# Bits issued from Pool, six operand tiles, new planner figures for a transpose, one hash in one pass, last store in halves

## The chip, the cores and the metric

The kernel runs on one core of one Trainium2 chip. The metric is the device time of one execution in microseconds (us). Before the change it is 277.95 us (median of three runs, 274.41 to 279.09). An execution that took over 1.5% more than the fastest of the same kernel is marked slow; the others are called fast. Every ratio below is the mean time of one kernel's fast runs over the mean time of the other kernel's fast runs of the same rounds on the same chip, so it is not quite the ratio of the medians that stand beside it. The interval behind it is a 95% interval.

## The reference

Hashed attention for 4 batches of 8 heads (768 tokens, head size 64), followed by a feed-forward network (FFN) with a maximum over three first layers:

```python
q_bits = (einsum('bhsd,dk->bhsk', q, proj) > 0)      # 6 bits; the same for k
mask = q_bucket[:, :, :, None] == k_bucket[:, :, None, :]
scores = where(mask, scale * q @ k.T, -1e9)          # softmax, then @ v
...                                                  # heads side by side: x is 3072 x 512
h = maximum(maximum(x @ w1, x @ w2), x @ w3)         # 512 -> 768
out = h @ w_out                                      # 768 -> 512
```

## The kernel before

Work goes by pairs of heads, four pairs in each batch; I write (1,2) for pair 2 of batch 1. A pair's q and k are loaded by SyncE, split into two fp16 parts by ScalarE and VectorE (tile `s`), and transposed into the operand tile `T`: the first six pairs on TensorE, the other ten by a DMA transpose from SBUF to SBUF. TensorE then hashes `T` (tile `hps`); VectorE makes bits of the hash. The bits go SBUF to HBM (`dr<-bt`) and from there into spare rows of `T` (`T<-dr`), so that the score matmul itself carries the mask. I call those two copies a bounce.

```python
def xbar(b, pr, e):                                   # the DMA transpose
    nc.sync.dma_start_transpose(operand(b, pr)[:], S16[b, pr][:].rearrange("p a d -> p (a d)"))
def bit_out(b, pr, e):
    ...
    nc.sync.dma_start(drs[b, pr][:].rearrange("n r t -> r n t"), bts.pop((b, pr))[:])
def bit_in(b, pr, e):
    nc.sync.dma_start(T[b, pr][D : D + NBITS, :, :], ...)
```

The order of the instructions on each engine is not written down. A list scheduler makes it at build time. Each task has a planned time on its engine; a DMA has a planned transfer time too (`xfer`). When an engine is free in the plan, the ready task of best priority is emitted. The plan says that a DMA has landed after its time on the engine, 0.3 us (2.4 for Pool), the transfer, and `POST` = 1.2 us.

```python
ev = [add(("SP", 2.0), p0 + 2, both_rs, lambda e: xbar(b, pr, e), xfer=4.3, take=("T",))]
...
hm = add(("PE", 1.3 if b == 0 else 0.67), p0 + 4, ev + [mp], lambda e: hash_mm(b, pr, (0, 2), e), take=("mm",))
...
stage = {(0, 3): [(1, 0)], (1, 0): [(1, 1), (1, 2)], (1, 1): ["o"]}   # weight loads, issued by Pool
# "o": nc.gpsimd.dma_start(wout_sb[:], ...) waits until the bits of (1,1) are in
```

So the plan takes a transpose to have landed 2.0 + 0.3 + 4.3 + 1.2 = 7.8 us after its issue, at the earliest (the plan lets transfers through one at a time), and places the hash of that pair accordingly. The last weight load, W_out, is 768 KB in fp16, cast by the DMA from 1536 KB of fp32, issued by Pool.

The softmax here doesn't subtract the row's maximum and nothing guards it: scores larger than these inputs give would overflow.

## Time and profile before

| what | before |
|---|---|
| median of the runs | 277.95 us |
| span of the profiled run (fast) | 272.9 us |
| TensorE busy | 260.2 us, 95% |
| hash waiting for transposes | 0.5 us |
| score waiting for bits | 2.3 us |
| half-clock intervals of TensorE inside the run | one, 3.4 us at 97 |

The first thing to read is TensorE's 95%: time can be won or lost only where TensorE stands still or has its clock halved. The prediction below shows the lines for this. (A chain there is the work that ended last, followed back from the last instruction, at each step to what released it. A DMA lands with its last completion record.) One more view is needed for what came later: SyncE's issues around 54 us (columns: start, how long the instruction held the queue, what was issued).

```profile
49.49 0.33 SPq L337 DMA_DIRECT2D dr<-bt  x1
54.62 4.36 SPq L271 DMA_TRANSPOSE T<-s  x1
59.15 0.35 SPq L340 DMA_DIRECT2D T<-dr  x1
...
63.90 5.12 SPq L445 DMA_TRANSPOSE xT<-xn  x1
```

The bits of (1,1) go out, the transpose of (1,2) is issued while they travel, then the bits come in. W_out is issued by Pool at 62.77, after that transpose has landed (61.01 by the completion records of the trace, 6.39 us after issue). The last line is the transpose of the FFN's input, half as large. It was issued 1.1 us after W_out and landed 11.19 us later; the six others of its kind landed in 3.65 to 5.26. Nothing waited for it at once, and I passed over it when I predicted.

### The profile page before, as it was taken

To read this page: it belongs to the slowest core of one execution; us is meant where nothing else is said; L and a number is where in the kernel's file an instruction comes from. 1 tells how busy PE (TensorE), PEld (TensorE's weight loads), DVE (VectorE), ACT (ScalarE), POOL (GpSimd) and SP (SyncE) were. 2 spreads that over 40 slices of the span, in tenths; PEclk is the share of its full clock that TensorE was granted. 3 is DMA by queue.
4 is the path that set the end of the run, shared out by engine and by line. 5 is a ranking of instruction groups with operands and counts; after the bars stand their busy time and mean duration, and the time that the engine had idled before them with its cause. 6 is when DMAs were issued, how large, how long until landed. Compare 5 with 4: busy or idle time off the path is not lost.

```text
span 272.9 us, 7413 instructions
## 1 busy us (share of the span) xinstructions
PE 260.2 (95%) x3034; PEld 175.1 (64%) x3034; DVE 176.7 (65%) x392; ACT 196.0 (72%) x282; POOL 37.9 (14%) x56
## 2 busy tenths in 40 slices
PE   7999989999999699899999999999999999999993
PEld 7878767667657365567667676666666656565551
DVE  4998598958958569766999466454356715354350
ACT  5797899999856178898999889998889432322322
POOL 1170042604303033030333000000000000000000
PEclk9999999999999979999999999999999999999998
DMA  7996496989999969999799950211250050120303
GB/s 206 350 221 112 137 268 180 148 143 324 204 288 237 155 234 234 260 204 278 193 208 263 198 116 8 34 26 41 77 60 4 0 155 20 40 79 0 115 0 116
DMA packets 67216, 40.51 MB, mean 148 GB/s; under 512 B 47982, under 2 KB 64110, under 8 KB 67182
## 3 DMA queue, kind: packets, MB, share of 16 engines
q1 hardware_dynamic: 63150, 36.90, 55.1%
q0 software_dynamic: 3952, 3.15, 7.9%
q8 instruction: 23, 0.38, 0.6%
q14 instruction: 11, 0.09, 0.1%
q10 hardware_dynamic: 80, 0.00, 0.0%
HBM read 25.72 MB, written 6.84 MB: 119 GB/s over the span
## 4 chain that ended last, share of the span: by engine, by line
PE 76%; DMA 11%; DVE 6%; ACT 4%; issue 1%; SPq 1%; ACTq 0%
PE ps L466 32%; PE sc L383 19%; PE po L480 10%; PE av L401 10%; DMA T<-s 6%; ACT AT L389 3%; DMA T<-dr 3%; DVE s L262 3%; PE hps L300 2%; DMA q<-in_q_dram 2%; PE tps L281 1%; PE hps L298 1%; DVE s L257 1%; DVE T L193 1%; ACT s L255 1%
## 5 line engine op out<-in xcount | busy, mean ns | idle before, releaser
L389 ACT ACTIVATE AT<-sc 128x768 f16<-128x768 f32 x192 | 146.1, 813 | 16.2 <-PE sc L383 15.1
L466 PE MATMUL ps<-xT,w_sb 128*128 128x384 f16 x576 | 107.1, 327 | 0.7 <-ACT ht L191 0.6
L383 PE MATMUL sc<-T 128*128 128x384 f16 x384 | 93.7, 327 | 3.5 <-DMA T<-dr 2.3
L475 DVE TENSOR_TENSOR ht<-ht,ps 128x384 f16<-128x384 f16 x96 | 53.0, 552 | 47.3 <-PE ps L466 43.8
L401 PEld LDWEIGHTS <-AT 128*128 128x128 f16 x1152 | 60.2, 98 | 24.3 <-issue 1.2
L466 PEld LDWEIGHTS <-w_sb 128*128 128x128 f16 x576 | 52.5, 98 | 30.9 <-issue 1.5
L401 PE MATMUL av<-vone,AT 128*128 128x65 f16 x1152 | 66.3, 193 | 0.3 <-DVE t L418 0.3
L383 PEld LDWEIGHTS <-T 128*128 128x128 f16 x384 | 30.1, 98 | 14.5 <-DMA T<-dr 2.9
L191 ACT CAST ht<-ps 128x384 f16<-128x384 f32 x30 | 14.4, 478 | 32.9 <-DVE ht L475 20.6
L480 PE MATMUL po<-wout_sb,ht 128*128 128x512 f16 x144 | 33.4, 379 | 0.0
L191 ACT COPY osb<-po 128x512 f32<-128x512 f32 x23 | 13.5, 585 | 18.5 <-PE po L480 18.4
L480 PEld LDWEIGHTS <-ht 128*128 128x128 f16 x144 | 13.6, 98 | 14.4
L418 DVE TENSOR_TENSOR t<-av,mv 128x390 f32<-128x390 f32 x32 | 17.9, 560 | 7.0 <-PE av L401 7.0
L351 POOL TENSOR_TENSOR vt<-v 128x384 f32<-128x384 f32 x12 | 12.9, 1073 | 63.8 <-DMA v<-in_v_dram 63.6
L262 DVE SCALAR_TENSOR_TENSOR s<-k,s 128x384 f16<-128x384 f32 x32 | 20.9, 665 | 0.7 <-ACT s L255 0.5
L262 DVE SCALAR_TENSOR_TENSOR s<-q,s 128x384 f16<-128x384 f32 x32 | 19.4, 620 | 2.9 <-ACT s L255 2.7
L193 DVE CAST ht<-ps 128x384 f16<-128x384 f32 x18 | 10.0, 556 | 15.2 <-PE ps L466 15.2
L437 DVE TENSOR_TENSOR xn<-t,rr 128x384 f16<-128x384 f32 x32 | 18.7, 584 | 1.1
L281 PE MATMUL tps<-iden,s 128*128 128x128 f16 x168 | 13.5, 219 | 1.5 <-DVE s L262 0.6
L281 PEld LDWEIGHTS <-s 128*128 128x128 f16 x168 | 10.5, 98 | 3.1 <-DVE s L262 1.8
L191 ACT CAST vone<-v 128x768 f16<-128x768 f32 x12 | 10.1, 839 | 0.0
L300 PEld LDWEIGHTS <-T 128*128 128x128 f16 x288 | 8.6, 96 | 1.9 <-DMA T<-s 1.1
(53 smaller groups left out, 141.8 us busy)
## 6 DMA issues: line engine op xcount, KB each, us to landing
v<-in_v_dram SPq DMA_DIRECT2D x16, 384.0 KB
out_dram<-osb SPq DMA_DIRECT2D x24, 256.0 KB
q<-in_q_dram SPq DMA_DIRECT2D x15, 384.0 KB
k<-in_k_dram SPq DMA_DIRECT2D x15, 384.0 KB
w_sb<-in_moe_w_dram POOLq DMA_DIRECT2D x6, 384.0 KB, 6.5
wout_sb<-in_moe_w_out_dram POOLq DMA_DIRECT2D x1, 768.0 KB, 11.5
dr<-bt SPq DMA_DIRECT2D x15, 36.0 KB
T<-dr SPq DMA_DIRECT2D x15, 36.0 KB
```

The lines of the kernel that those rows point to most:

```text
L191: nc.scalar.copy(o, i)
L262: nc.vector.scalar_tensor_tensor(out=s[:, a0:a1, D : 2 * D], in0=raw_view(n, b, pr, heads), scalar=QS, in1=s[:, a0:a1, 0:D], op0=AluOp.mul ...
L281: nc.tensor.transpose(p16[:, c * P : (c + 1) * P], S16[b, pr][:, a0 + c, :], iden[:])
L300: nc.tensor.matmul(o, T[b, pr][:, a, :], PAB[:], start=True, stop=True)
L383: nc.tensor.matmul(sc[:, i, 0:HQ], t[:, NA2 + hh * NCH + 2 * j + i, :], t[:, hh * NCH + hf * CH : hh * NCH + (hf + 1) * CH, :], start=True ...
L389: nc.scalar.activation(AT[:], scs.pop(u)[:, :, 0:HQ], ActFn.Exp, bias=EXP_BIAS, scale=EXP_SCALE)
L401: nc.tensor.matmul(av[:, o : o + D + 1], AT[:, i, c * P : (c + 1) * P], vones[b % 2][:, 2 * pr + hh, 2 * j + i, 0 : D + 1], start=slot == ...
L418: nc.vector.tensor_tensor(out=t[:, :, :, 0 : D + 1], in0=av[:, :, :, 0 : D + 1], in1=mv, op=AluOp.add)
L437: nc.vector.tensor_tensor(out=xv, in0=t[:, :, :, 0:D], in1=rr[:].to_broadcast([P, 2, CH, D]), op=AluOp.mult)
L466: nc.tensor.matmul(ps[:, 0:HQ], w_sb[i][:, jc, fb * P : (fb + 1) * P], xTs[b, hf][:, jc, :], start=jc == 0, stop=jc == NJ - 1)
L475: nc.vector.tensor_tensor(out=ht[:], in0=ht[:], in1=ps[:, 0:HQ], op=AluOp.max)
L480: nc.tensor.matmul(ps[:], hts[b, hf, fb][:, c * P : (c + 1) * P], wout_sb[:, fb, :], start=fb == 0, stop=fb == NF - 1)
```

## The change

The intent: take the bits of the later pairs off SyncE, where they queue behind transposes; tell the planner that a transpose occupies SyncE for 4.3 us; use less SBUF for operand tiles; halve the matmuls of one hash; shorten the tail.

```diff
-    OSB = 3
+    OSB = 5
-    opnd = ... bufs=8        # and "T": 8 in the plan
+    opnd = ... bufs=6        # and "T": 6
-        K = NBITS if b == 0 else 2 * NBITS
+        summed = 4 * b + pr < 3          # (0,3) is now hashed in one pass
+        K = NBITS if summed else 2 * NBITS
-        nc.sync.dma_start(drs[b, pr]...          # bit_out, bit_in
+        ENG[e].dma_start(drs[b, pr]...
+    POOL_FROM = 6
-            ev = [add(("SP", 2.0), p0 + 2, both_rs, lambda e: xbar(b, pr, e), xfer=4.3, take=("T",))]
+            ev = [add(("SP", 4.3), p0 + 2, both_rs, lambda e: xbar(b, pr, e), xfer=0.4, take=("T",))]
-        hm = add(("PE", 1.3 if b == 0 else 0.67), ...
+        hm = add(("PE", 1.3 if 4 * b + pr < 3 else 0.67), ...     # hash bits: 0.3 -> 0.62 likewise
+        mover = ("POOL", 0.9) if 4 * b + pr >= POOL_FROM else ("SP", 0.65)
-        bo = add(("SP", 0.65), ...                                # and bi
+        bo = add(mover, ...
-        for c in range(CH):
+        for c in range(CH) if (b, hf) != (B - 1, 1) else (0, 1, 2.1, 2.6):    # last output tile in halves
... (cut: the bodies for halves of an output tile)
```

The planned landing of a transpose falls from 7.8 to 4.3 + 0.3 + 0.4 + 1.2 = 6.2 us. Since transfers pass one at a time in the plan, other DMAs behind a transpose are planned sooner too.

## The prediction

> **What bounds the kernel now.** I read the page's shares first, then the time stretch by stretch, then the chain of waits, then the groups inside the stretches that lose time, last the order of issues on SyncE. The shares:
>
> ```profile
> PE 260.2 (95%) x3034; PEld 175.1 (64%) x3034; DVE 176.7 (65%) x392; ACT 196.0 (72%) x282; POOL 37.9 (14%) x56
> ```
>
> TensorE is busy 95% of the span, so a change elsewhere can only give back what TensorE loses. To see where it loses, I cut the span in stretches (columns: stretch and its length, then PE, PEld, DVE, ACT, POOL busy us with instruction counts, granted clock, DMA share, GB/s):
>
> ```profile
> 10.00:25.00 15.00, 14.43 (x301) 12.33 (x299) 14.42 (x32) 12.42 (x18) 5.86 (x7) 1.00 1.02 239
> 25.00:50.00 25.00, 23.28 (x390) 17.80 (x387) 20.01 (x50) 23.33 (x34) 6.86 (x11) 1.00 0.69 182
> 50.00:85.00 35.00, 34.70 (x392) 22.80 (x389) 26.81 (x60) 29.70 (x44) 10.00 (x14) 1.00 1.02 219
> 85.00:100.00 15.00, 12.35 (x128) 7.59 (x126) 10.09 (x22) 5.16 (x9) 2.05 (x4) 0.90 0.90 200
> 110.00:125.00 15.00, 13.98 (x202) 9.60 (x201) 10.93 (x25) 13.56 (x21) 2.33 (x3) 1.00 1.17 239
> 125.00:160.00 35.00, 35.00 (x475) 24.32 (x473) 28.12 (x63) 31.68 (x45) 6.78 (x9) 1.00 1.01 226
> 160.00:268.60 108.60, 108.56 (x952) 66.98 (x950) 51.92 (x104) 64.61 (x96) 0.00 (x0) 1.00 0.17 45
> ```
>
> Busy time flatters, since matmul ends are modelled. So I counted the matmuls of each stretch and multiplied by the pace at which the chain shows them end to end: 0.327 us for two of score, 0.65 for four of the first FFN layer, 0.184 for six of attend, 1.29 for six of the second layer, 0.58 for 24 of the one-pass hash. From 160 on this gives 108.9 us of work in 108.6 us: full, nothing to win. 50 to 85 and 125 to 160 are full too. What is lost: 1.0 us in 10 to 25, 4.0 in 25 to 50, **4.3 in 85 to 100** (10.7 of work in 15), **1.8 in 110 to 125**. Together 11.1 us, beside about 9 of start-up and the tail.
>
> The two bold losses in the chain (start, length, what):
>
> ```profile
> 90.30 0.71 PE ps L466 x4
> 91.02 4.86 DMA T<-dr
> 95.93 0.82 PE sc L383 x4
> ...
> 102.93 8.01 DMA T<-s
> 110.99 0.76 PE hps L300 x24
> ...
> 113.96 9.39 DMA T<-s
> 123.40 0.76 PE hps L300 x24
> ```
>
> At 95.9 the first score of the eighth pair (batch 1, pair 3) waits for its hash bits, which travel SBUF to HBM and back. After that idling the 5-us stretch 95 to 100 runs at a granted clock of 0.69 with 2.7 us of work in it; TensorE was idle 0.93 us in that stretch, so the clock alone took about 1.3. Why the bits are late stands in SyncE's issue order:
>
> ```profile
> 78.44 6.35 SPq L271 DMA_TRANSPOSE T<-s  x1
> 84.84 1.43 SPq L489 DMA_DIRECT2D out_dram<-osb  x2
> 86.38 0.56 SPq L337 DMA_DIRECT2D dr<-bt  x1
> 87.05 3.87 SPq L271 DMA_TRANSPOSE T<-s  x1
> 91.02 0.41 SPq L340 DMA_DIRECT2D T<-dr  x1
> ```
>
> The outbound bits stand behind a transpose that holds the queue for 6.35 us and behind two stores; their completion record comes 2.75 us after issue (89.1), but the inbound copy stands behind another transpose of 3.87 us and then needs 4.86 us itself. An undisturbed bounce in this trace (out at 162.6, in at 164.1) lands after 1.45 and 2.33 us. The hash waits at 111.0 and 123.4 are another thing: they wait for the transposes themselves.
>
> **What the Trainium skill says.** "DMA: Bandwidth & Descriptors", section "Issuing engines are not separate DMA queues": starting DMAs from several engines saves only the starting sequencer's time, usually a small thing. The trace differs in size: a transpose holds SyncE for 3.7 to 6.4 us, so here that time is the point. The same page, section "Queues, rings and completion order": SP has its own row of rings and each DMA engine takes turns between rows, so bits from Pool need not stand behind SyncE's packets; no trace yet shows that. "SBUF — State Buffer", section "SBUF: two separate sides": Pool's descriptors can be starved while VectorE holds the shared port in a two-port mode. The seven weight loads issued from Pool took 0.75 to 0.92 us, beside a VectorE that was mostly busy: no sign of it. "TensorE: Matmul & The Clock Gate", Part 1: an idle TensorE is put on half clock, in windows of 3413 ns. Agrees: the trace's clock record has one half-clock interval of 3.413 us at 97.
>
> **The change part by part.** I compared the emitted orders and measured, in TensorE work at the paces above, how much lies between the transpose of a pair's bits and that pair's first score.
>
> *Bounces from Pool (pairs 6 to 15), and a schedule that knows that a transpose holds SyncE 4.3 us.* 20 issues leave SyncE (327 + 287 ns a pair, 6.1 us in all) and cost Pool about 20 x 0.79 = 16 us (the mean of a weight load's issue), on an engine busy 38 of 273: not on the path. Pair (1,3), the one that stalls, had 10.9 us between bits and score and gets 16.0; (1,2) had 14.4 and gets 11.5; every later one has 15.7 or more. Pair (1,1) stays on SyncE but no longer has a transpose between its two copies. Bounce needed: 0.5 VectorE + 0.8 issue + some 3 landing + 0.8 issue + some 3 landing, about 8 us. So (1,3) no longer waits: I credit its idle 2.0 us and 1.3 of clock. The 0.9 left of the 4.3 is FFN evictions, kept. **-3.3.**
>
> *Six operand tiles for eight.* In a later batch four tiles are live and two prefetch. A tile is freed a batch-half before its successor is needed, so no score starves, but it gates the transposes: (2,2), (2,3), (3,2) and (3,3) start their transpose 5 to 14 us of TensorE work later than their split. Between the earliest start of a transpose and its hash the new order leaves 8.5 to 13.9 us, seven of ten under 10. A transpose lands 6.4 to 9.4 us after issue in this trace. The old order had 9.2 to 12.6 and lost 1.8. I expect slightly more such waits: **+0.9.**
>
> *Hash of (0,3) in one pass.* 24 matmuls for 48: 1.18 us becomes 0.58. VectorE pays 300 + 307 ns instead of 299. Both fall in 25 to 50, where ScalarE is busy 23.3 of 25 and TensorE already has 4 us spare, so I count half: **-0.3.**
>
> *Five output tiles, last store in halves.* Five tiles: no wait on an output tile is on the path. Halves: six matmuls of 512 become twelve of 256, the same time. The last eviction, 585 ns for 512 columns against 478 for 384 on the same engine, so 0.84 ns a column, falls to about 0.37: 0.2 saved. The last store carries half (2.0 us landing for 256 KB, 1.45 for 36 KB): 0.3 saved. **-0.5.**
>
> Sum: -3.3 + 0.9 - 0.3 - 0.5 = -3.2 us.
>
> **Rivals.**
> First, hash waits take the place of the score wait. For it: TensorE takes its work in order, the hash slack is shorter than before for most pairs, and DMA is near full from 65 to 160 (share about 1). Against: bounces leave SyncE, so transposes issue sooner. If seven transposes lose 0.7 us each, it is +4.9 less the 1.8 there is: the gain is gone, near 277.5.
> Second, Pool's order becomes the new blockage. Pool waits 63.6 us for value loads in nine waits, up to 12.8; a bounce put behind such a sum inherits the wait. In the new order four of the Pool bounces have the sum of a later pair between out and in. For (1,2), with 11.5 us, a late value tile would bring the old stall back: 3 us, near 277. Against: that tile's load stands directly behind the first transpose in SyncE's order, 17 us of TensorE work before its sum, and the later pairs have slack to spare.
> Third, everything works: no waits after 50, all 6.1 us of the two bold losses back, plus 0.8: 7 us, near 270. ScalarE speaks against the whole of it: 31.7 of 35 busy in 125 to 160, so work pulled forward meets an engine that is nearly full.
>
> **Range and chances.** The three runs before are 274.41, 277.95 and 279.09, the profiled one 274.82 with a span of 272.9. Waits on DMA are what can differ from one run to the next, and so can the clock window that follows a wait; fewer waits should help the slow runs more. From the median 277.95, minus 3.2, minus about 1.5 for that: **273.2**. Low 269.8 (third rival and quiet runs), high 277.2 (first or second). Faster by over 2% means under 272.4: 0.38. Within 2%: 0.58. Slower needs both rivals at once: 0.04.
>
> **What would show it.** In the profile after: no transfer of bits on the chain before the scores between 85 and 100, no half-clock interval inside the run, and lost TensorE time there near 1 us. Bits issued by Pool in about 0.8 us, landing in 2 to 4. Waits of the hash for transposes 2 to 3 us in sum; over 5 and the first rival won. Pool waiting for a value tile with bits queued behind it, and a score waiting for them: the second. The last store's eviction near 0.37 us. I am wrong if the chain shows a transpose wait of over 1.5 us, or if 125 to 160 is no longer full.

## The result

| | before | changed |
|---|---|---|
| median | 277.32 us (4 runs, 274.41 to 279.09) | 290.69 us (4 runs, 288.24 to 294.36) |
| ratio of fast runs | | 1.0489 [1.0352, 1.0627]: slower |
| span of the profiled run | 272.9 us | 292.6 us |

The changed kernel is 4.9% slower, where I had expected 1.7% faster. Its profiled run took 294.36 us and counts as slow (2.1% above the fastest run); its fast runs took 288.24, 290.45 and 290.93. So some 4 us of the profile's span are more than usual. What I read from it returns in fast profiles of the experiments.

The shares of the changed kernel:

```profile
PE 264.4 (90%) x3016; PEld 177.4 (61%) x3016; DVE 175.7 (60%) x388; ACT 199.9 (68%) x288; POOL 50.9 (17%) x76
```

TensorE's share fell from 95% to 90%. The stretches of the changed kernel that answer to those in the prediction (stretch and its length, then PE, PEld, DVE, ACT and POOL busy, granted clock, DMA share, GB/s):

```profile
25.00:50.00 25.00, 22.80 (x372) 17.60 (x371) 19.89 (x49) 23.79 (x34) 5.10 (x9) 1.00 0.60 170
50.00:85.00 35.00, 21.70 (x235) 13.94 (x233) 19.63 (x42) 20.45 (x29) 10.46 (x15) 0.88 1.13 164
85.00:100.00 15.00, 14.57 (x148) 9.03 (x149) 5.93 (x15) 6.54 (x11) 2.01 (x3) 0.83 0.66 152
110.00:125.00 15.00, 13.38 (x169) 9.01 (x168) 12.22 (x27) 12.25 (x17) 4.22 (x7) 1.00 0.65 118
125.00:160.00 35.00, 32.02 (x397) 21.50 (x396) 25.28 (x55) 27.40 (x39) 10.62 (x15) 0.95 1.04 226
```

The stretch 50 to 85 was full before and now holds 235 matmuls instead of 392. It is the hole. Counting the matmuls at their chain pace, as in the prediction, TensorE loses here:

| stretch | lost before, us | lost after, us |
|---|---|---|
| 10 to 50 | 5.0 | 5.1 |
| 50 to 85 | 0.3 | 15.6 |
| 85 to 100 | 4.3 | 2.5 |
| 100 to 125 | 1.7 | 2.4 |
| 125 to 160 | -0.4 | 5.1 |

The sum goes from 10.9 to 30.7 us, a difference of 19.8; the spans differ by 19.7. So this table has all of the loss. Waits of TensorE in the changed kernel (us in total, times, longest):

```profile
PE hps L301 <- DMA T<-s: 13.9, 4, 7.7
```

Before, this line read 0.5 us, once. Most of the rest of the loss is clock: TensorE's clock record has half-clock intervals of 6.8 us at 73.2 and 83.4 and of 3.4 us at 138.0, each in or behind one of these waits, against one of 3.4 us before. Half of the TensorE busy time inside these intervals, an estimate of what they cost, is 6.0 us against 1.7. Small waits moved as well; that of scores for ScalarE's tile `AT` grew from 0.9 to 3.7 us. The chain of the changed kernel around the three waits (start, length, what):

```profile
49.83 6.93 DMA dr<-bt
...
66.16 2.34 DMA q<-in_q_dram
68.50 16.88 DMA T<-s
85.43 0.81 PE hps L301 x24
...
127.97 8.87 DMA T<-s
136.89 0.76 PE hps L301 x24
```

A transpose that took 6.4 to 9.4 us before needs 16.88 us here. SyncE's and then Pool's issues in the changed kernel:

```profile
56.90 0.29 SPq L341 DMA_DIRECT2D T<-dr  x1
...
58.75 7.35 SPq L271 DMA_TRANSPOSE T<-s  x1
...
68.50 13.28 SPq L271 DMA_TRANSPOSE T<-s  x1
```

```profile
60.25 1.23 POOL L647 DMA_DIRECT2D wout_sb<-in_moe_w_out_dram  x1 [0.28 <-issue]
```

The order has flipped. Before, the transpose of (1,2) stood between the two copies of the bits of (1,1). Now it stands behind both and behind the next pair's loads, and W_out follows 1.5 us after it, because W_out too starts when those bits are in:

```
before:   bits(1,1) out   T(1,2)          bits(1,1) in   loads(1,3)  loads(2,0)   | Pool: W_out
changed:  bits(1,1) out   bits(1,1) in    loads(1,3)     T(1,2)  | Pool: W_out |  loads(2,0)  T(1,3)
```

By the completion records the transpose of (1,2) landed after 17.5 us, W_out after 18.91 (11.46 before), three loads after 12.7 to 13.7, and the transpose of (1,3), which could not be issued before the first one let go, after 16.88. Two cuts of 5 us from that time:

```profile
70.00:75.00 5.00, 0.00 (x0) 0.00 (x0) 0.00 (x0) 0.00 (x0) 0.00 (x0) 0.82 1.39 106
75.00:80.00 5.00, 3.70 (x46) 2.66 (x47) 0.76 (x3) 1.02 (x2) 0.00 (x0) 0.50 1.24 275
```

For 5 us no engine does anything while DMA is full (share 1.39) and moves only 106 GB/s. Then TensorE comes back at half clock.

### The profile page after: what moved, and what is told of

Read it like the earlier page. It is cut to its first block, busy times and chain, and to the rows that moved or that the text cites.

```text
span 292.6 us, 7393 instructions
## 1 busy us (share of the span) xinstructions
PE 264.4 (90%) x3016; PEld 177.4 (61%) x3016; DVE 175.7 (60%) x388; ACT 199.9 (68%) x288; POOL 50.9 (17%) x76
## 4 chain that ended last, share of the span: by engine, by line
PE 57%; DMA 23%; DVE 12%; ACT 3%; issue 2%; SPq 1%; ACTq 0%
PE ps L467 24%; PE sc L384 12%; DMA T<-s 11%; PE po L485 10%; DMA q<-in_q_dram 8%; PE av L402 7%; DVE s L262 5%; DMA dr<-bt 3%; DVE s L257 2%; DVE ht L476 2%; ACT s L255 1%; PE hps L301 1%; ACT AT L390 1%; PE tps L281 1%; DVE xn L438 1%
## 5 line engine op out<-in xcount | busy, mean ns | idle before, releaser
L390 ACT ACTIVATE AT<-sc 128x768 f16<-128x768 f32 x192 | 146.0, 812 | 19.7 <-PE sc L384 18.9
L467 PE MATMUL ps<-xT,w_sb 128*128 128x384 f16 x576 | 109.0, 330 | 1.3 <-DVE ht L476 0.9
L384 PE MATMUL sc<-T 128*128 128x384 f16 x384 | 95.2, 331 | 4.3 <-ACT AT L390 3.7
L402 PEld LDWEIGHTS <-AT 128*128 128x128 f16 x1152 | 61.8, 99 | 25.8 <-issue 2.9
L402 PE MATMUL av<-vone,AT 128*128 128x65 f16 x1152 | 67.7, 195 | 0.0
L384 PEld LDWEIGHTS <-T 128*128 128x128 f16 x384 | 30.7, 98 | 15.7 <-issue 5.3
L485 PE MATMUL po<-wout_sb,ht 128*128 128x512 f16 (+1 forms) x150 | 33.4, 370 | 0.0
L262 DVE SCALAR_TENSOR_TENSOR s<-q,s 128x384 f16<-128x384 f32 x32 | 20.8, 656 | 8.5 <-ACT s L255 8.3
L191 ACT COPY osb<-po 128x512 f32<-128x512 f32 (+1 forms) x24 | 13.6, 567 | 17.0 <-PE po L485 16.8
L301 PE MATMUL hps<-PAB,T 128*128 128x12 f16 x312 | 9.8, 169 | 14.1 <-DMA T<-s 13.9
L438 DVE TENSOR_TENSOR xn<-t,rr 128x384 f16<-128x384 f32 x32 | 19.7, 615 | 1.1
L255 ACT ACTIVATE s<-q 128x768 f16<-128x768 f32 (+1 forms) x10 | 7.8, 778 | 15.8 <-DMA q<-in_q_dram 13.9
L301 PEld LDWEIGHTS <-T 128*128 128x128 f16 x312 | 9.1, 97 | 15.5 <-DMA T<-s 14.9
## 6 DMA issues: line engine op xcount, KB each, us to landing
wout_sb<-in_moe_w_out_dram POOLq DMA_DIRECT2D x1, 768.0 KB, 18.9
```

The costliest lines, as they stand in the source:

```text
L191: nc.scalar.copy(o, i)
L262: nc.vector.scalar_tensor_tensor(out=s[:, a0:a1, D : 2 * D], in0=raw_view(n, b, pr, heads), scalar=QS, in1=s[:, a0:a1, 0:D], op0=AluOp.mul ...
L301: nc.tensor.matmul(o, T[b, pr][:, a, :], PAB[:], start=True, stop=True)
L384: nc.tensor.matmul(sc[:, i, 0:HQ], t[:, NA2 + hh * NCH + 2 * j + i, :], t[:, hh * NCH + hf * CH : hh * NCH + (hf + 1) * CH, :], start=True ...
L390: nc.scalar.activation(AT[:], scs.pop(u)[:, :, 0:HQ], ActFn.Exp, bias=EXP_BIAS, scale=EXP_SCALE)
L402: nc.tensor.matmul(av[:, o : o + D + 1], AT[:, i, c * P : (c + 1) * P], vones[b % 2][:, 2 * pr + hh, 2 * j + i, 0 : D + 1], start=slot == ...
```

## The experiments

Sixteen kernels ran. My theories, in the order in which I formed them: first, that the one-pass hash flips the order, and that the flip makes the transposes meet W_out; the rivals were Pool's bounces and the six tiles. Then, that the new planner figures (4.3 and 0.4 us) place each hash too soon after its transpose. Where an expectation uses letters, A is the first theory and C the one of the figures; others are the rivals it describes.

### First round: is it the flip?

**e1: the changed kernel without the one-pass hash.**

```diff
-        summed = 4 * b + pr < 3        # and the planned times likewise
+        summed = b == 0
```

> The changed kernel with the hash of batch 0 pair 3 put back to two passes, all else as changed. Built orders show why this is asked: that one part flips SyncE's order, so that the transpose of pair (1,2) stands in front of the inbound bits of (1,1) again instead of behind them and behind three loads, and the output-weight load from Pool comes after it. Theory A (the flipped order, with the output-weight load running into the transposes, costs the time): hash waits for transposes fall from 13.9 us to under 4, no transpose lands later than 10 us after issue, time 272 to 278 us. Theory B (six tiles or bounces from Pool cost the time): it stays near 288 to 291.

Measured: 280.23 us, ratio 1.0194 [1.0093, 1.0294], profile span 278.0. SyncE's order is that of before again, and no operand transpose takes over 9.3 us. So more than half of the loss is gone. But the hash waits are not under 4 us as I had expected. They are 8.6 us in five waits:

```profile
PE hps L301 <- DMA T<-s: 8.6, 5, 3.3
```

With the order restored, something else still makes hashes wait.

**e2: the kernel before with the one-pass hash alone.** The edit is the `summed` part of the diff above.

> The kernel before with only the one-pass hash of batch 0 pair 3. Theory A: the same flip of SyncE's order, so slow by itself: 284 to 294 us, with a transpose landing 14 us or more after issue near 60 us of the span. Theory B: within 1% of before, about 277 us.

Measured: 279.74 us, ratio 1.0142 [1.0066, 1.0217]. The flip is there: the transpose of (1,2) at 57.19 landed after 14.22 us, that of (1,3) at 66.33 after 13.54. One hash wait of 5.8 us follows, and 6.8 us of half clock at 70.5. This single part of the change, which I had booked as a gain of 0.3 us, costs 1.4%. It costs less than I expected here (284 to 294 us): with the old figures no other hash waits for a transpose in its profile.

**e3: the changed kernel with W_out issued earlier,** between the other weight loads near 38 us, in the same order otherwise.

```diff
+        if (i, half) == (0, 1):                      # in load_w
+            nc.gpsimd.dma_start(wout_sb[:], ...)
-                           lambda e: nc.gpsimd.dma_start(wout_sb[:], ...),
+                           lambda e: None,
```

> The changed kernel, same order of everything on all engines, except that Pool issues the output-weight load (768 KB) about 22 us earlier, right behind the weight load at 37 us, away from the transposes. Theory A1 (it is the overlap of this load with the transposes): transposes near 58 and 68 us land 6 to 9 us after issue, hash waits under 5 us, time 274 to 280. Theory A2 (it is the late transpose itself: inbound bits and loads ahead of it, two transposes in a row): transposes still land late, time stays 285 or more.

Measured: 287.31 us, but three of four runs were slow and the one fast run took 282.63, so there is no ratio. The first two transposes landed in 8.6 and 8.9 us, without the collision, but they were issued only at 63.2 and 71.6: the earlier load pushed the other weight loads and the bits of (1,1) back. The time of this run is confounded and I do not use it.

**e4: the kernel before with W_out moved into the first transpose,** by the same edit at a later weight load.

> The kernel before, same order, except that Pool issues the output-weight load about 14 us earlier, right behind two weight loads at 47 us, so that it is in flight when the transpose of (1,2) is issued at about 54.6 us. Theory A1: that transpose lands 11 us or more after issue instead of 6.4, the hash of (1,2) waits, time 3 to 10 us longer (280 to 287). Theory A2: transpose lands in under 8 us, time within 1% of before.

Measured: 275.37 us, ratio 0.9992 [0.9924, 1.006]. The edit missed: W_out ran from 49.42 to 60.40 and the transpose was issued at 57.11, so they shared 3 us, and the transpose landed after 7.91. It says nothing on a full overlap. The two on their own follow in e11.

### Second round: one part at a time

**e5: the kernel before with the new figures alone.**

```diff
-            ev = [add(("SP", 2.0), ..., xfer=4.3, take=("T",))]
+            ev = [add(("SP", 4.3), ..., xfer=0.4, take=("T",))]
```

> The kernel before with only the planner's figures for a transpose changed (SyncE 4.3 us and 0.4 us of transfer instead of 2.0 and 4.3), so the order that the changed kernel's planner makes, all else as before. In its built order the hash follows the earliest start of its transpose by 8.0 to 8.8 us of TensorE work for six of ten pairs (9.2 to 12.6 before). Theory C (the new figures plan the hash before the transposes land): the hash waits for transposes more: TensorE's waits on transposes rise from 0.5 us to 4 or more, time 278 to 283. Rival D (figures harmless, hash flip is all): within 1% of before.

Measured: 284.56 us (one of the four runs slow), ratio 1.0298 [1.0208, 1.0388]. The profiled run is fast. Its waits:

```profile
PE hps L301 <- DMA T<-s: 7.0, 4, 2.9
```

Its transposes land in 5.5 to 9.6 us (6.4 to 9.4 before). No transfer became much slower; the hash was placed nearer. Counted in the traces at the paces above, TensorE's work between the issue of a transpose and its hash is 4.9 to 8.8 us here, 6.5 in the mean, where it was 6.2 to 9.5 and 8.2. (The slack in the expectation is counted in the built order from the splits on.) Behind two of the waits the clock halves, at 78.5 and 157.0. Two numbers in the planner cost 3.0%.

**e6: the kernel before with Pool's bounces alone** (`POOL_FROM = 6`).

> The kernel before with only the bounces of pairs 6 to 15 issued from Pool. Theory C and D: the score wait and half-clock interval near 96 us go, bits land in 3 to 5 us, time 1 to 2% shorter, 270 to 274. Theory B (bounces from Pool cost the time): 280 or more, with scores waiting for bits or Pool busy behind value tiles.

Measured: 277.64 us, ratio 1.0067 [0.9991, 1.0143]. The score wait near 96 is gone, and the stretch 85 to 100 loses 2.1 us instead of 4.3. But 100 to 125 loses 6.0 instead of 1.7. What the profile wins in one stretch it loses in the next, and the time is not the 270 to 274 us that I had expected. A new wait and a half-clock interval at 109.8 stand there:

```profile
PE av L402 <- DVE t L419: 1.5, 1, 1.5
```

One hash also waits 1.7 us for its transpose, against 0.5 before.

**e7: the kernel before with six operand tiles alone.**

> The kernel before with only six operand tiles for eight. Theory C and D: within 1% of before (275 to 278); the stall near 96 us stays, since its pair comes before the tiles bind. Theory B' (six tiles cost the time): 280 or more, with score or hash waits after 100 us.

Measured: 276.56 us, ratio 1.0008 [0.9911, 1.0105]. The tiles cost nothing that the runs resolve, about 1% either way. The other half of the expectation failed: the stall near 96 us did not stay, though the bits still go through SyncE and stand behind a transpose. SyncE's issues, and TensorE at 95 to 100 (busy all of it, at full clock):

```profile
88.89 0.47 SPq L338 DMA_DIRECT2D dr<-bt  x1
89.46 4.08 SPq L271 DMA_TRANSPOSE T<-s  x1
93.64 0.41 SPq L341 DMA_DIRECT2D T<-dr  x1
```

```profile
95.00:100.00 5.00, 5.00 (x63) 3.39 (x61) 3.44 (x8) 3.24 (x6) 0.00 (x0) 1.00 0.82 240
```

e7's order differs a little from that of before. But e4, e12 and e15 have SyncE's order of before unchanged, and TensorE's too but for e12's shorter hash. Scores wait for bits 2.3 us in the profile before, and not at all, 0.5 and 0.4 us in these three; none has a half-clock interval near 97. This is e12's line:

```profile
PE sc L384 <- DMA T<-dr: 0.5, 1, 0.5
```

And of the 28 executions of the kernel before that were timed beside the experiments, 23 were granted a mean clock of 0.996 or more. One half-clock interval of 3.4 us in a span of 273 takes the mean to 0.994, so these 23 had none inside. The stall that the bounces from Pool were to remove belonged to the profiled execution more than to the kernel.

**e8: the changed kernel with two-pass hash and the old figures (2.0 and 4.3).** What is left are Pool's bounces, six tiles, five output tiles and the halved store.

> The changed kernel with two parts put back: the two-pass hash of batch 0 pair 3 and the old planner figures for a transpose; bounces from Pool, six tiles, five output tiles and the split last store stay. Theory C with A: both harmful parts gone, hash waits under 2 us in sum, no half-clock interval inside the run, time 270 to 274, faster than before. Theory B: still 278 or more.

Measured: 277.02 us, ratio 1.0025 [0.994, 1.0109]. The whole loss has gone, with the hash waits (0.4 us). Taken one at a time, the parts sum to nearly the whole: flip 1.4, figures 3.0, rest 0.25, together 4.7% against 4.9% measured. They do not sum in every grouping: e1 holds the figures and the rest and costs 1.9%, less than the figures alone in e5, though the intervals overlap. That the bounces bring nothing shows here too: I had expected 270 to 274 us and no half-clock interval inside the run, and there is one at 109.8. The chain of e8:

```profile
89.74 1.57 SPq L271
...
91.38 5.04 DMA q<-in_q_dram
...
101.67 0.81 DVE s L262
...
108.27 0.48 DVE t L419
...
108.80 0.34 PE av L402 x6
```

The bits no longer stand behind the transpose; the loads of the next pairs still do. The load at 91.38 follows a transpose that held SyncE. Its splits on VectorE then come so late that VectorE reaches the addition that frees the attend bank only at 108.27, and TensorE waits. I took it that this lateness did not show in the kernel before because TensorE stood still for the bits in that time. e4 speaks against that: in the order of before, its TensorE does not wait for bits, and by the same count it loses only about 2.5 us in 100 to 125. What makes VectorE late here stays open.

### Third round: separate the figures, the overlap and the operation

**e9: the changed kernel with one figure changed,** the planned transfer of a transpose.

```diff
-            ev = [add(("SP", 4.3), ..., xfer=0.4, take=("T",))]
+            ev = [add(("SP", 4.3), ..., xfer=4.3, take=("T",))]
```

> The changed kernel with one figure changed: the planner is told 4.3 us of transfer for a transpose in place of 0.4 (SyncE stays at 4.3), so a hash is planned 10 us after its transpose is issued in place of 6. The one-pass hash and its flipped order stay. Theory C: the waits of the hash for transposes after 100 us go, and those on the first two shrink; TensorE's waits on transposes fall from 13.9 us to 3 to 8, time 278 to 284, in place of 290.7. If the figure is not the cause, it stays at 287 or more.

Measured: 277.2 us (one run slow), ratio 1.0035 [0.9939, 1.0131]. SyncE's order in e9 still has the flip:

```profile
57.49 6.47 SPq L271 DMA_TRANSPOSE T<-s  x1
...
65.77 11.61 SPq L271 DMA_TRANSPOSE T<-s  x1
```

These two transposes still land after 14.6 and 13.7 us, W_out after 16.0. Yet the hash waits are

```profile
PE hps L301 <- DMA T<-s: 0.9, 1, 0.9
```

because more TensorE work stands between the issue of a transpose and its hash: 8.8 to 12.5 us counted in the trace, against 3.3 to 8.5 in the changed kernel, and over 12 for the two slow ones. This is the most telling run: the slow landing need not become a hash wait; with the short figure it does. It is not free where it stands: by the same count TensorE still loses about 6 us in 50 to 85, in other waits of up to 1.2 us. The whole time is that of before within the interval, up to 1.3% more.

**e10: two-pass hash and 4.3 + 2.7,** meant as a version to beat both kernels.

> Candidate to beat both: the changed kernel with the two-pass hash put back and a transpose planned as SyncE 4.3 us and 2.7 us of transfer, near what the traces show (8.5 us from issue to landing with the planner's fixed parts). Theory C with A: hash waits under 1 us, 271 to 276, not slower than before. If loads that bunch up on SyncE and late VectorE work bind, as near 105 us in the run with the old figures, it is again within 1% of before.

Measured: 275.08 us, ratio 0.9975 [0.9895, 1.0054]: the same as before. It has no half-clock interval inside the run, and still no gain. Its largest wait is for the addition that frees the attend bank (2.8 us in three waits).

**e11: the collision by itself.** A kernel that only issues loads of W_out and the same transpose, phase after phase, each phase after the one before has landed, three times over. Its output is wrong, which doesn't matter for the time. It is one run of unknown state, 240.47 us; the phases are compared within it.

```python
for _ in range(3):
    phase([], True)                     # the transpose alone
    phase(["pool_cast"], False); phase(["pool_cast"], True)     # W_out as in the kernel; with transpose
    phase(["pool_plain"], False); phase(["pool_plain"], True)   # fp32, no cast, 1536 KB written
    phase(["act"], False); phase(["act"], True)                 # the same, issued by ScalarE
```

> Not the computation (wrong result on purpose: the outputs are ones): three rounds of seven phases, one after the other: a transpose of 128x3072 alone; the output-weight load from Pool with cast to fp16, alone and beside a transpose; the same from Pool without cast, alone and beside one; the same without cast from ScalarE's queue, alone and beside one. Theory A1 (a load in flight from Pool holds the transpose up): alone the transpose lands 5.5 to 6.5 us after issue, beside the load with cast 10 us or more. If it is the bytes, all three loads hold it up alike; if it is Pool's descriptors, the two from Pool do more than the one from ScalarE; if it is the cast, the one with cast alone. Rival A2: beside any of them under 8 us.

The chain of the first round (time from issue to landing of what ended last in a phase):

```profile
4.10 5.53 DMA T<-s
...
10.18 7.33 DMA w_cast<-in_moe_w_out_dram
...
18.09 14.35 DMA T<-s
...
41.20 18.81 DMA T<-s
...
67.87 9.90 DMA T<-s
```

| | load | transpose |
|---|---|---|
| transpose alone | | 5.45 to 5.53 |
| Pool, cast, alone | 7.2 to 7.3 | |
| Pool, cast, both | 14.0, 10.1, 10.1 | 14.35, 8.93, 8.96 |
| Pool, no cast, alone | 7.4 | |
| Pool, no cast, both | 18.4 to 18.9 | 18.8 to 19.4 |
| ScalarE, same bytes as the row above, alone | 6.7 to 6.9 | |
| ScalarE, both | 7.5 | 9.9, three times |

Beside a load issued by Pool, each of the two can take longer than both one after the other would (19 us against 5.5 + 7.4). The same bytes from ScalarE's queue cost the transpose 4.4 us and the load under 1. So neither the bytes nor the cast alone makes it; it goes with Pool as the issuer. What about Pool's loads does it is not separated. Their packets have another size (4096 bytes each without the cast, 2048 from ScalarE), and they were issued 0.08 to 0.37 us after the transpose, ScalarE's load 0.05 to 0.18 us before it; no run exchanges either. The moment counts: in the two milder cast phases the transpose was 0.37 us ahead of the load, in the first 0.09.

**e12: the kernel before, one-pass hash executed but planned with the old times.** Only `summed` and the choice of the bits' function differ, so the order stays that of before.

> The kernel before with the one-pass hash executed for batch 0 pair 3, but planned with the old durations (1.3 us on TensorE, 0.3 on VectorE), so the built order on every engine is that of before. Theory A (the order, not the operation, cost 1.4%): within 0.5% of before, 275 to 277. If the operation itself costs (its second VectorE instruction), 278 or more.

Measured: 276.74 us, ratio 1.0064 [0.9995, 1.0134]. The transposes land after at most 10.1 us and the one hash wait is 0.8 us, where e2 had 5.8: that wait came with the flip and not with the operation. The times alone do not part the two runs, since their intervals overlap. The ratio is slightly above my half per cent, with 1.0 in the interval; the hoped-for gain of 0.3 us is not there.

### Fourth round: how much is the overlap, and where the bounces' gain went

**e13: the changed kernel with W_out cut to a sixth** (wrong output).

```diff
-  lambda e: nc.gpsimd.dma_start(wout_sb[:], moe_w_out.rearrange(...)),
+  lambda e: nc.gpsimd.dma_start(wout_sb[:, 0:1, :], moe_w_out[0:P, :].rearrange(...)),
```

> The changed kernel in the same order, with the output-weight load cut to a sixth (128 KB for 768; the rest of the tile is zeros, so the result is wrong on purpose). If the overlap of that load with the transposes is part of the loss: the two transposes near 58 and 68 us land in 6 to 10 us instead of 17, waits of the hash fall from 13.9 us to under 7, time 280 to 285. If not: landings fall but the time stays at 288 or more.

Measured: 281.45 us, ratio 1.0202 [1.0145, 1.0258]. The two transposes land after 10.39 and 9.25 us, and the waits shrink:

```profile
PE hps L302 <- DMA T<-s: 6.0, 3, 3.5
```

13.9 to 6.0 us of waits, 4.9% to 2.0%. So about 2.9 points (8 us of 276) come from the overlap with W_out, and the rest from hashes that are placed too near to ordinary transposes, as in e1.

**e14 and e15: the sums of value tiles on Pool cut short,** in e8's kernel and in the kernel before. VectorE's splits read two SBUF inputs; "SBUF — State Buffer", section "Who interferes with whom" in the Trainium skill, says that such an instruction contends with a Pool instruction that reads SBUF. The traces agree: a split beside a value sum takes 0.92 us on average in e8 (up to 1.96), one without 0.58; before it is 0.83 against 0.59. I suspected that this is where the bounces' gain went. The edit replaces three Pool additions by one small copy; it computes something else, though the result stayed within tolerance.

> The changed kernel with the two-pass hash and old figures, and Pool's three-instruction value sum replaced by one copy of one column (wrong result on purpose, same order). If Pool's sums, by slowing VectorE's splits, took the gain of the bounces: no split over 0.9 us, TensorE's loss at 100 to 125 us falls from 4.9 to 2 or less, time 271 to 273.5, 1 to 2% under before. If the bunched loads alone do it: 275 to 277.

> Control: the kernel before with the same short sum (wrong result on purpose). The score wait near 96 us is not touched by VectorE's splits, so 274 to 277, within 1% of before; if it falls as far as the run beside it, the sum costs both kernels alike and says nothing about where the gain of the bounces went.

Measured: 273.1 us, ratio 0.9895 [0.9839, 0.9952] for e14; 273.29 us, ratio 0.9889 [0.9841, 0.9937] for the control. In e14 TensorE's loss in 100 to 125 fell from about 5.0 to 3.3 us, not to the 2 that I had named. Even so, without the control I would have called the suspicion confirmed. With it, it falls: the sums cost both kernels the same 1.1%, and do not explain why bounces from Pool gain nothing.

**e16: two-pass hash and 4.3 + 4.3,** the widest figures.

> The changed kernel with the two-pass hash and a transpose planned as SyncE 4.3 us and 4.3 us of transfer. No hash waits (under 0.5 us); 273 to 276, same as before or up to 1% faster.

Measured: 275.49 us, ratio 0.9977 [0.9935, 1.0018], the same as before. No correct version beat the kernel before by a margin that the runs resolve; e10 and e16 are both 0.25% below it, within their intervals.

## Why the prediction was wrong

**The bound and the tail: right.** TensorE is the bound; the lost TensorE time accounts for the whole difference of the spans. The last eviction takes 0.37 us (0.58 before), and the last store lands after 1.70 us instead of 2.00: 0.5 us, as predicted.

**"Six operand tiles for eight: +0.9": the step that failed.** Two things were wrong in it. First, the heading: e7 shows that the tiles cost nothing that the runs resolve. The shorter slack that I worked out there came from the planner's figures, which I had read as "a schedule that knows that a transpose holds SyncE 4.3 us" and not as a landing planned 1.6 us sooner. Alone they cost 3.0% (e5), some 8 us. I had the slack, "8.5 to 13.9 us, seven of ten under 10", and the landing, "6.4 to 9.4", side by side, and took their small difference for enough. Second, the ends of the comparison. I counted the slack "between the earliest start of a transpose and its hash", that is from its splits, but SyncE reaches the transpose of (1,2) only behind the inbound bits of (1,1), which wait 6.93 us for the outbound copy, and behind three loads. And the landing range came from a trace in which no operand transpose ran beside the whole of W_out; beside it they took 17.5 and 16.88 us. The overlap is worth 2.9 of the 4.9 points in this kernel (e13). How much it costs depends on the figure: nothing that the runs resolve with a landing planned 10.1 us after issue (e9), 1.4% with the old 7.8 (e2).

**The hash in one pass, "-0.3": wrong in kind.** I priced the operation. Its cost is in the order: the halved planned time shifts the plan just enough to flip SyncE's list, +1.4% (e2), while the operation with the old order is within noise (e12). I had the new order of issues at hand and looked in it for slack before scores, not for new neighbours of a transpose.

**Bounces from Pool, "-3.3": there was hardly a wait to remove.** The score wait near 96 is gone where bounces moved (e6, e8), but it is gone or 0.5 us at most where they did not (e4, e7, e12, e15), and 23 of 28 other executions of the kernel before had no half-clock interval inside. I priced 2.0 us of idling and 1.3 of clock from one profile, as if every execution had them. That the bounces bring nothing measurable fits this (e6: 1.0067 [0.9991, 1.0143]). Pool's issues took 0.65 to 0.73 us, less than the predicted 0.79, and landed in 2.0 to 5.8. In the profiles of e6 and e8, 100 to 125 lost about what 85 to 100 gained. That the loads which still stand behind a transpose and the late VectorE work are on the path there is what their chains show; why is not shown. The value sums are ruled out as the difference (e15). This part stays open.

**The rivals.** The first rival, that hash waits take the score wait's place, is what happened, at 13.9 us of waits instead of its 4.9. Its estimate also had no term for the clock behind long waits: 17.1 us of half-clock intervals against 3.4. (Its own sum was loose: -3.3 - 0.3 - 0.5 + 3.1 is -1.0, so 277.0 and not 277.5.) The second rival, Pool's order as a blockage, did not appear. The chance of 0.04 for slower rested on needing "both rivals at once"; one was enough.

The marks that I had named did their work: hash waits over 5 us, a transpose wait of over 1.5 us in the chain, and 125 to 160 no longer full are all in the profile.

## What to carry to other kernels

When a scheduler makes the order, a changed planning figure is a change of the kernel: compare the emitted orders first for who now stands beside whom in time, and only then price the operations. A planned landing that is too short on an engine that takes its work in order becomes idle time on each transfer that is later than planned; one that is generous costs little, as the single figure in e9 shows. Before the removal of a wait is priced, look whether the wait is there in a second execution: here a profile of any close variant, or the granted clock of the repeated runs, would have told. And before a range of durations from a trace is used, look for the one record of a similar transfer under the new conditions: here the FFN transpose with 11.19 us beside W_out was in the trace of the kernel before.

## What the Trainium skill lacked or had wrong

- "DMA: Bandwidth & Descriptors", section "Rules for kernel authors", says that a transpose next to ordinary DMAs "needs nothing". That is about correctness, and no run contradicts it there (e9, with the same overlap, gave correct results). What it lacks is the price: a transpose that lands in 5.5 us alone took 9.9 us beside a 1536 KB load from ScalarE's queue, and 9 to 19 us beside loads from Pool, which were slowed to 10 to 19 us from 7.3 themselves.
- The same page, section "Issuing engines are not separate DMA queues", treats the issuing engine as a matter of sequencer time. Here the same bytes from Pool and from ScalarE differed by 9 us in what they did to a transpose beside them (19 against 9.9 us); packet size and the order of issue differed too.
- The same page counts the sequencer's cycles of a DMA transpose only in a table that sets trn3 against generations it does not name. No page gives the time on this chip, or that it grows beside other traffic: a transpose held SyncE for 3.64 to 7.35 us in the changed kernel, and 13.28 us when one was issued while another was still slow beside a Pool load.
- "TensorE: Matmul & The Clock Gate", Part 1, agrees: every half-clock interval of these traces that ended inside the run lasted 3.413 or 6.827 us, one or two of its windows.
